# Cosine of the MLP input as a sine of the unfolded angle, with a bound from norms computed on the chip

## The chip, the cores and the metric

One core of one Trainium2 chip. The time is device microseconds of one launch: the median of three runs of the kernel before is 1383.35 us (1379.19 to 1383.68). The profile comes from one execution, whose span from first to last instruction is 1382.2 us, 1.15 us below that median. Engines are named as in the profile: PE (matmul, with PEld for its weight loads), DVE (vector), ACT (activation functions), POOL (GpSimd) and SP, which here issues DMAs only.

## What is computed

Three stages follow each other:

```python
# 1. attention, 4 batches x 8 heads, 576 positions, head size 64: only the 32 largest scores of a row count
scores = q @ k.T / 8;  kth = 32nd largest of each row
attn = softmax(scores where scores >= kth);  x = (attn @ v) laid out as 2304 tokens x 512
# 2. an MLP with an unusual activation
h = x @ w_in          # 2304 x 2048
g = h * np.cos(h)
x = g @ w_out         # 2304 x 512
# 3. eight experts, one per token (argmax of a gate), 512 -> 1024 -> 512
out[token] = gate_weight * eom * (relu(x @ w1[e]) @ w2[e])
```

The inputs fix the sizes that matter below: w_in is drawn as normal numbers divided by the root of 512, so a column of it has a squared length near 1 (its standard deviation is the root of 2/512, or 0.06), and a row of x is a mean of some 32 rows of v, which are normal numbers times 0.1, so its squared length is near 512 x 0.01 / 32 = 0.16.

## The kernel before

The work is a list of operations, each with its engine, an estimated duration, the values it reads and writes, and a due time (`prio`). A planner in the program (`Plan`) takes this list before launch, gives each engine the most urgent operation that can start by its own estimates, and writes one fixed order for every engine. On the chip each engine goes through its own order, in order, waiting on semaphores. The tags of the planner (`hs`, `rr`, `nn`, `ps` and so on) are sets of places in memory: an operation can start only when its value has a place.

Attention goes by 80 units: 64 main units (128 query rows of two heads) and 16 mixed ones (64 rows of two heads). In a unit PE makes the scores (L551), ACT copies them out of the banks (L557), DVE folds a row into maxima and minima of its halves (L580) and finds the 32nd largest value with MAX8 and MATCH_REPLACE8 (L585 to L600), POOL and ACT turn the rest into a large negative number (L604 to L618), ACT takes the exponential (L621), DVE makes the reciprocals and spreads them (L627, L629), and PE turns and multiplies with v (L641 to L682). The result, split into a high and a low part of reduced precision, goes into one of two places `xc`, a chunk of 256 tokens. There are 9 chunks.

As soon as a chunk is whole, the MLP runs on it, in 8 units of 256 tokens x 256 columns of w_in (72 units in all), interleaved with the attention of the next chunks. Each unit, `moe_unit`: 24 matmuls (L765 to L767; high x high, high x low, low x high), ACT copies the bank to `hs` (L771), POOL computes h/(2 pi) + 1/4 into `rr` (L773), DVE rounds that to an integer in `nn` by adding and subtracting a large constant (L775), POOL subtracts (L777). Units are collected in groups of up to four, and ACT takes the sine of 2 pi times the folded fraction of a whole group (L787), because exponential and sine need different tables, and each change of table shows as a load of 1283 ns. `moe_tail` then multiplies with h (DVE, L795), splits (ACT L806, POOL L808) and multiplies with w_out, whose tiles SP loads again and again from a scratch buffer (PE, L816 to L818). When the eighth unit of a chunk is done, `route` works out the expert of each token.

Beside this, in the first 330 us, the double-precision weights w_in and w_out are narrowed (L714 to L749) by DVE, ACT and POOL. The tag `nn` serves those too. After the last chunk, from about 1086 us on, the experts run; PE is busy nearly all of that stretch. A one-time check stands between the two: DVE reduces the flags of ties in the top 32 to one number per partition, PE adds it and the counts of tokens over the partitions (L1111, L1112), and DVE writes the result (L1116, L1117). At the very end a branch reads it: if a number exceeds the capacity, a slow general path recomputes what is needed, in plain loops that fold the angle as above.

Banks of PSUM: six are shared by everything before the experts (`ps`), two hold the w_out sums (`acc`).

Of the kernel before, what the change touches and what calls it, by code (L numbers as in the profile page):

```python
# [8 lines left out]
F32 = mybir.dt.float32  # L9
# [4 lines left out]
AF = mybir.ActivationFunctionType  # L14
OP = mybir.AluOpType
AX = mybir.AxisListType

P = 128
TOPK = 32
MAGIC = 12582912.0  # L20
INV_2PI = 0.15915494309189535
TWO_PI = 6.2831850
LOWEST = -3.0e38
MASK_GAIN = float(2.0 ** 90)
FAR = 1 << 20
# [41 lines left out]


class Buf:
    """A value in one of the places of its tag; the place is picked when the first op starts."""  # L70

    def __init__(self, tag, dt):
        self.tag = tag
# [11 lines left out]


class Plan:
    """Orders the ops of all engines: takes them in program order, finds what depends on what,
    and gives each engine the most urgent op that can start."""

    CROSS = 190.0
    SAME = {"PE": 0.0, "ACT": 130.0, "DVE": 130.0, "POOL": 130.0, "SP": 0.0}
# [4 lines left out]
        self.loose = set()  # L97

    def tag(self, name, places, loose=False, under=None):
        """`places`: (ap, area, first, last) each; `under`: tags whose last values must have left the place."""  # L100
        if loose:
            self.loose.add(name)
        self.tags[name] = []
        for ap, area, lo, hi in places:
            below = [(n, p) for n in under or () for p in self.tags[n] if p[3] == area and p[4] < hi and lo < p[5]]
            self.tags[name].append([ap, 0.0, True, area, lo, hi, below])
# [35 lines left out]
        return o  # L142

    def gone(self, slot):
        """When the values under a place are gone, or None."""
        t = slot[1]
        for n, p in slot[6]:
            if not p[2] or self.taken[n] < len(self.line[n]):
                return None
            t = max(t, p[1])  # L150
        return t

    def place(self, o, t):
        """When the places that `o` needs are free, or None."""
        need = {}
        for b in o.bufs:
            if b.tag and b.slot is None:
                need.setdefault(b.tag, []).append(b)
        for tag, bs in need.items():
            if tag not in self.loose:  # L160
                head = self.line[tag][self.taken[tag]:self.taken[tag] + len(bs)]
                if any(b not in head for b in bs):
                    return None
            free = sorted(f for f in (self.gone(s) for s in self.tags[tag] if s[2]) if f is not None)
            if len(free) < len(bs):
                return None
            t = max(t, free[len(bs) - 1])
        return t
# [78 lines left out]
def vec(n, psum=False):  # L247
    return 69.0 + n * (1.04 if psum else 1.042)


def fast(n):
    return 69.0 + n * 0.521
# [6 lines left out]
def pool(n):  # L259
    return 20.0 + n * 2.357  # L260


def pool_s(n):
    return 80.0 + n * 0.98
# [3 lines left out]
def tile_topk_attention_moe_moe2(ctx, tc, q, k, v, w_in, w_out, w_gate, w_ogate, w1, w2, out):  # L268
# [42 lines left out]
    seen = const.tile([P, E], F32, name="seen")  # L311
    nc.gpsimd.memset(seen, 0.0)
    spacer = const.tile([1, 1], F32, name="spacer")
    ebias = const.tile([P, 2], F32, name="ebias")
    nc.gpsimd.memset(ebias[:, 0:1], float(-EXP_OFF * 2 ** 23))
    nc.gpsimd.memset(ebias[:, 1:2], float(2 ** 20))

    tiles = []
    for b in range(B):
# [128 lines left out]
    plan.tag("ps", banks[0:6], loose=True)  # L448
    plan.tag("acc", banks[6:8])

    B_wg, B_table, B_x2d, B_seen, B_out = (plan.fixed() for _ in range(5))
    B_wod = plan.fixed()

    def dma(fn, nbytes, r=(), w=(), prio=0.0):
# [300 lines left out]

    def moe_unit(c, fp, prio):
        xc = XC[c]
        ph, hs, rr, nn = plan.buf("ps"), plan.buf("hs"), plan.buf("rr"), plan.buf("nn")
        for i in range(2):
            for c_ in range(KC):  # L760
                def mm(i=i, c_=c_):
                    o = ph.ap[:, i * CH:(i + 1) * CH]
                    fs = slice((2 * fp + i) * P, (2 * fp + i + 1) * P)
                    xh, xl = xc.ap
                    nc.tensor.matmul(o, w_in_h[:, c_, fs], xh[:, c_, :], start=(c_ == 0), stop=False)  # L765
                    nc.tensor.matmul(o, w_in_h[:, c_, fs], xl[:, c_, :], start=False, stop=False)  # L766
                    nc.tensor.matmul(o, w_in_l[:, c_, fs], xh[:, c_, :], start=False, stop=(c_ == KC - 1))  # L767

                plan.op({"PE": 327.0}, mm, [xc] + [(B_win, (fp // 2, c_, t)) for t in range(2)],
                        [ph], prio, hold=[hs])  # L770
        plan.op({"ACT": act(512, psum=True)}, lambda: nc.scalar.activation(hs.ap, ph.ap, AF.Copy),  # L771
                [ph], [hs], prio)
        plan.op({"POOL": pool_s(512)}, lambda: nc.gpsimd.tensor_scalar(  # L773
            rr.ap, hs.ap, INV_2PI, 0.25, op0=OP.mult, op1=OP.add), [hs], [rr], prio)
        plan.op({"DVE": fast(512)}, lambda: nc.vector.tensor_scalar(  # L775
            nn.ap, rr.ap, MAGIC, MAGIC, op0=OP.add, op1=OP.subtract), [rr], [nn], prio)
        plan.op({"POOL": pool(512)}, lambda: nc.gpsimd.tensor_tensor(rr.ap, rr.ap, nn.ap, op=OP.subtract),  # L777
                [nn], [rr], prio)
        group.append((c, fp, hs, rr, prio))
        if len(group) == SINS or (c, fp) in SIN_ENDS or (c, fp) == (NTILE // 2 - 1, UPC - 1):  # L780
            g = list(group)
            group.clear()
            rrs = [x[3] for x in g]

            def sins():
                for x in rrs:
                    nc.scalar.activation(x.ap, x.ap, AF.Sin, scale=TWO_PI)  # L787

            plan.op({"ACT": len(rrs) * 520.0}, sins, [], rrs, prio, kind="sin")
            for x in g:  # L790
                tail_at[0] = max(tail_at[0] + 10.0, prio + ADD["tail"])
                moe_tail(*x[:4], tail_at[0])

    def moe_tail(c, fp, hs, rr, prio):
        plan.op({"DVE": vec(512)}, lambda: nc.vector.tensor_tensor(rr.ap, hs.ap, rr.ap, op=OP.mult),  # L795
                [hs], [rr], prio)
        if fp == 0:
            ACC[c] = [plan.buf("acc"), plan.buf("acc")]
        acc = ACC[c]
        for i in range(2):  # L800
            f = 2 * fp + i
            ghl, wl = plan.buf("ghl"), plan.buf("wl", F32R)
            dma(lambda f=f, wl=wl: nc.sync.dma_start(shaped(wl.ap, 2, DM), wod[f]), P * 4096, r=[(B_wod, f)],
                w=[wl], prio=prio + 3 * i)
            gv = lambda i=i: rr.ap[:, i * CH:(i + 1) * CH]
            plan.op({"ACT": act(CH)}, lambda gv=gv, ghl=ghl: nc.scalar.activation(ghl.ap[:, 0], gv(), AF.Copy),  # L806
                    [rr], [(ghl, 0)], prio + 3 * i)
            plan.op({"POOL": pool(CH)}, lambda gv=gv, ghl=ghl: nc.gpsimd.tensor_tensor(  # L808
                ghl.ap[:, 1], gv(), ghl.ap[:, 0].bitcast(F32), op=OP.subtract), [rr, (ghl, 0)], [(ghl, 1)],
                prio + 3 * i)  # L810
            for t in range(2):
                def mm(f=f, t=t, ghl=ghl, wl=wl):
                    wr = lambda s: wl.ap[:, s * DM:(s + 1) * DM].bitcast(F32R)
                    ts_ = slice(t * P, (t + 1) * P)
                    gh, gl = ghl.ap[:, 0, ts_], ghl.ap[:, 1, ts_]
                    nc.tensor.matmul(acc[t].ap, gh, wr(0), start=(f == 0), stop=False)  # L816
                    nc.tensor.matmul(acc[t].ap, gh, wr(1), start=False, stop=False)  # L817
                    nc.tensor.matmul(acc[t].ap, gl, wr(0), start=False, stop=(f == NF - 1))  # L818

                plan.op({"PE": 648.0}, mm, [ghl, wl], [acc[t]], prio + 3 * i, hold=[acc[1 - t]])  # L820
        if fp == UPC - 1:
            route(c, prio + 1)
# [114 lines left out]
    for u in range(NU):  # L937
        if u in firsts:
            load_heads(*firsts[u], 10.0 * u - LOAD_AHEAD)
        attention(u)  # L940
        while todo and (u in chunk_done and todo[0] or len(pieces) - len(todo) < CONV_RATE * (u + 1)):
            f, a = todo.pop(0)
            f(*a, CONV_AT + 10.0 / CONV_RATE * (len(pieces) - len(todo)))
        if u in chunk_done:
            c = chunk_done[u]
            for fp in range(UPC):
                moe_unit(c, fp, 10.0 * (ready[c] + MOE_LAG) + MOE_STEP * fp)

# [146 lines left out]
    for e in range(E):  # L1095
# [10 lines left out]
            [B_flags], [B_worst], base)  # L1106
    plan.op({"DVE": 80.0}, lambda: nc.vector.tensor_scalar(
        worst[:, 1:2], worst[:, 0:1], 0.0, float(CAP + 1), op0=OP.is_ge, op1=OP.mult), [], [B_worst], base)

    def count():  # L1110
        nc.tensor.matmul(pc.ap[:, 0:E], ones, seen, start=True, stop=True)  # L1111
        nc.tensor.matmul(pc.ap[:, E:E + 1], ones, worst[:, 1:2], start=True, stop=True)  # L1112

    B_cnt = plan.fixed()
    plan.op({"PE": 120.0}, count, [B_seen, B_worst], [pc], base)
# [273 lines left out]
```

## Time and profile before

| | |
|---|---|
| median of three runs | 1383.35 us |
| profiled execution, span | 1382.2 us |
| PE busy | 1180.1 us, 85% |
| PE weight loads busy | 936.6 us, 68% |
| DVE busy | 988.5 us, 72% |
| ACT busy | 854.9 us, 62% |
| POOL busy | 885.2 us, 64% |
| first and last fold subtraction (L777) | 162.7 us, 1034.1 us |

Busy time is the union of an engine's instructions. Matmuls overlap each other, so their busy time and their single durations are longer than their spacing. In a list of groups, the columns are: line, engine, operation, output and input, shapes, count; then busy time in us and the mean of one in ns; then the idle time of the engine just before them and what ended it.

### The profile page before, as it was taken

What the parts mean: (1) busy time and instruction counts of PE and PEld (TensorE: products, weight loads), DVE (VectorE), ACT (ScalarE), POOL (GpSimd) and SP (SyncE); (2) the same over time, 40 slices, a digit from 0 to 9 for tenths busy, and PEclk for the clock granted to TensorE, in tenths of its full rate; (3) what the DMA queues carried; (4) which work ended last, traced back from release to release, by engine and by line L of the source; (5) the groups of instructions that cost most, each with busy time, mean ns of one, the idle gap of its engine ahead of it and who ended that gap; (6) DMA issues with size and microseconds to landing.
All of it is one profiled execution on the core that took longest, in us unless ns stands there. A gap on an engine that the chain in (4) does not pass through costs nothing.

```text
span 1382.2 us, 22655 instructions
## 1 busy us (share of the span) xinstructions
PE 1180.1 (85%) x7478; PEld 936.6 (68%) x7479; DVE 988.5 (72%) x2864; ACT 854.9 (62%) x1854; POOL 885.2 (64%) x1130
## 2 busy tenths in 40 slices
PE   3467778768898999999989898899994599999996
PEld 2334555547677668668767676767883599999995
DVE  6999999779599888999987889888335234444410
ACT  5777777767577787777766668767555244444421
POOL 6778888888666865776676657766765455555400
PEclk9655779989999989999999999999996699999998
DMA  8223323534440343323345321241557444444100
GB/s 210 76 107 113 98 67 116 182 131 162 144 139 8 111 140 105 122 92 104 96 135 152 100 78 36 89 137 46 174 184 267 166 160 158 149 156 160 58 17 23
DMA packets 95807, 164.72 MB, mean 119 GB/s; under 512 B 49850, under 2 KB 54202, under 8 KB 95680
## 3 DMA queue, kind: packets, MB, share of 16 engines
q1 hardware_dynamic: 91264, 153.71, 34.3%
q0 software_dynamic: 4416, 9.47, 2.1%
q8 instruction: 61, 1.00, 0.3%
q14 instruction: 66, 0.54, 0.1%
HBM read 146.72 MB, written 19.56 MB: 120 GB/s over the span
## 4 chain that ended last, share of the span: by engine, by line
PE 41%; DVE 29%; POOL 13%; issue 10%; ACT 6%; DMA 2%; POOLq 0%; DVEq 0%; ACTq 0%
DVE area_a L590 7%; DVE area_a L595 6%; DVE area_a L580 6%; PE bank L682 4%; PE bank L551 3%; PE bank L816 3%; PE bank L818 3%; PE bank L817 3%; PE bank L1052 2%; PE bank L1053 2%; PE bank L641 2%; PE bank L1054 2%; POOL area_a L618 2%; PE bank L765 2%; POOL area_g L777 2%
## 5 line engine op out<-in xcount | busy, mean ns | idle before, releaser
L590 DVE MAX8 area_a<-area_a 128x8 f32<-128x288 f32 x576 | 243.6, 444 | 1.1
L618 POOL TENSOR_TENSOR area_a<-area_a 128x576 f32<-128x576 f32 x144 | 195.8, 1368 | 23.0 <-ACT area_a L614 21.9
L595 DVE MATCH_REPLACE8 area_a<-area_a 128x288 f32<-128x288 f32 x432 | 187.8, 438 | 0.0
L580 DVE TENSOR_TENSOR area_a<-area_a 128x288 f32<-128x288 f32 x288 | 176.7, 639 | 14.5 <-ACT area_a L557 11.0
L765 PE MATMUL bank<-area_f,area_w 128*128 128x256 f32 x576 | 177.6, 308 | 2.3 <-ACT area_h L771 2.3
L641 PE MATMUL bank<-ident,area_a 128*128 128x128 f32 x576 | 104.5, 313 | 70.6 <-ACT area_a L621 57.8
L766 PE MATMUL bank<-area_f,area_w 128*128 128x256 f32 x576 | 163.3, 284 | 0.0
L767 PE MATMUL bank<-area_f,area_w 128*128 128x256 f32 x576 | 163.0, 283 | 0.0
L551 PE MATMUL bank<-area_a 64*128 64x288 f32 x512 | 133.3, 513 | 25.5 <-ACT area_a L541 22.5
L641 PEld LDWEIGHTS bank<-ident,area_a 128*128 128x128 f32 x576 | 73.8, 158 | 100.3 <-ACT area_a L621 78.4
L816 PE MATMUL bank<-area_l,area_f 128*128 128x512 f32 x288 | 130.4, 453 | 1.3 <-ACT area_f L806 0.6
L614 ACT ACTIVATE area_a<-area_a 128x576 bf16<-128x576 f32 x144 | 107.3, 768 | 37.5 <-POOL area_a L604 37.2
L808 POOL TENSOR_TENSOR area_f<-area_g,area_f 128x256 fp32r<-128x256 f32 x144 | 114.9, 811 | 23.7 <-ACT area_f L806 20.8
L777 POOL TENSOR_TENSOR area_g<-area_g,area_n 128x512 f32<-128x512 f32 x72 | 105.7, 1468 | 35.3 <-DVE area_a L600 14.8
L621 ACT ACTIVATE area_a<-area_a 128x576 f32<-128x576 f32 x144 | 111.2, 773 | 27.1 <-POOL area_a L618 26.2
L682 PE MATMUL bank<-area_a 128*64 128x128 f32 (+3 forms) x1600 | 123.3, 296 | 1.5 <-ACT area_a L662 1.3
L818 PE MATMUL bank<-area_l,area_f 128*128 128x512 f32 x288 | 119.7, 416 | 5.3 <-POOL area_f L808 5.0
L765 PEld LDWEIGHTS bank<-area_f,area_w 128*128 128x128 f32 x576 | 112.1, 195 | 14.2 <-issue 9.2
L682 PEld LDWEIGHTS bank<-area_a 128*64 128x64 f32 (+1 forms) x1600 | 89.8, 150 | 42.3 <-issue 18.3
L817 PE MATMUL bank<-area_l,area_f 128*128 128x512 f32 x288 | 118.2, 410 | 0.0
L766 PEld LDWEIGHTS bank<-area_f,area_w 128*128 128x128 f32 x576 | 111.8, 194 | 1.0
L767 PEld LDWEIGHTS bank<-area_f,area_w 128*128 128x128 f32 x576 | 111.0, 193 | 0.0
(197 smaller groups left out, 3005.4 us busy)
## 6 DMA issues: line engine op xcount, KB each, us to landing
area_l<-wod SPq DMA_DIRECT2D x144, 512.0 KB, 3.6
area_l<-in_moe_w_dram SPq DMA_DIRECT2D x52, 512.0 KB, 4.3
area_l<-in_moe_w_in_dram SPq DMA_DIRECT2D x16, 512.0 KB, 4.3
area_l<-in_moe_w_out_dram SPq DMA_DIRECT2D x16, 512.0 KB, 4.1
wod<-area_l SPq DMA_DIRECT2D x16, 512.0 KB, 2.6
area_n<-in_moe_w_dram SPq DMA_DIRECT2D x12, 512.0 KB, 4.9
area_a<-in_k_dram SPq DMA_DIRECT2D x32, 128.0 KB, 3.5
area_a<-in_q_dram SPq DMA_DIRECT2D x32, 128.0 KB, 3.4
```

The source lines that it names most:

```text
L551: nc.tensor.matmul(o.ap[:, 0:HALF], qt.ap[j * D:(j + 1) * D, :], kt.ap[j * D:(j + 1) * D, at:at + HALF], start=True, stop=True)
L580: plan.op(cost, lambda j=j, to=to, op=op, eng=eng: eng.tensor_tensor(to(), sc.ap[:, j, 0:HALF], sc.ap[:, j, HALF:S], op=op), [(sc, j)], [( ...
L590: lambda j=j, t=t: nc.vector.max(mx.ap[:, j, 8 * t:8 * t + 8], up.ap[:, j, :]),
L595: lambda j=j, t=t: nc.vector.match_replace(up.ap[:, j, :], mx.ap[:, j, 8 * t:8 * t + 8], up.ap[:, j, :], LOWEST),
L618: plan.op({"POOL": 1234.0}, lambda j=j: nc.gpsimd.tensor_tensor(sc.ap[:, j, :], sc.ap[:, j, :], bl.ap[:, j, :], op=OP.subtract), [(bl, j)] ...
L641: nc.tensor.transpose(pp.ap[:, r_ * P:(r_ + 1) * P], flat[:, at + r_ * P:at + (r_ + 1) * P], ident)
L682: nc.tensor.matmul(o.ap[j * D:(j + 1) * D, 0:w], lh, rh, start=(r_ == 0), stop=(r_ == R))
L765: nc.tensor.matmul(o, w_in_h[:, c_, fs], xh[:, c_, :], start=(c_ == 0), stop=False)
L766: nc.tensor.matmul(o, w_in_h[:, c_, fs], xl[:, c_, :], start=False, stop=False)
L767: nc.tensor.matmul(o, w_in_l[:, c_, fs], xh[:, c_, :], start=False, stop=(c_ == KC - 1))
L816: nc.tensor.matmul(acc[t].ap, gh, wr(0), start=(f == 0), stop=False)
L818: nc.tensor.matmul(acc[t].ap, gl, wr(0), start=False, stop=(f == NF - 1))
```

## The change

The fold goes: L773, L775 and L777 are no longer there. The sine of a group reads `hs` itself, with the constant pi/2 added inside the activation as a bias read from a column of `ebias`, and writes `rr`. A place of `rr` is therefore taken when the sines start, not when the fold starts, and `nn` is used by the narrowing of weights alone.

[...] New products make a bound: for each chunk, PE multiplies the two 128-token blocks of the high part of x with themselves (4 matmuls each), and DVE takes the largest element of each row; in chunks 1 to 4 the same is done for four 128-column blocks of w_in. The diagonals are squared lengths. With x below 1.60 and w below 1.50, |h| is at most the root of 2.4, 1.549. Two new comparisons in the one-time check send the launch to the general path otherwise; they are added by two more one-column matmuls into the sum that the branch reads. The general path itself stays as it was.

```diff
-    ebias = const.tile([P, 2], F32, name="ebias")
+    ebias = const.tile([P, 3], F32, name="ebias")
...
+    nc.gpsimd.memset(ebias[:, 2:3], HALF_PI)
+    norms = const.tile([P, 2, NTILE // 2], F32, name="norms")
+    nc.gpsimd.memset(norms, 0.0)
...
     def moe_unit(c, fp, prio):
         xc = XC[c]
-        ph, hs, rr, nn = plan.buf("ps"), plan.buf("hs"), plan.buf("rr"), plan.buf("nn")
+        ph, hs, rr = plan.buf("ps"), plan.buf("hs"), plan.buf("rr")
...
-        plan.op({"POOL": pool_s(512)}, lambda: nc.gpsimd.tensor_scalar(
-            rr.ap, hs.ap, INV_2PI, 0.25, op0=OP.mult, op1=OP.add), [hs], [rr], prio)
-        plan.op({"DVE": fast(512)}, lambda: nc.vector.tensor_scalar(
-            nn.ap, rr.ap, MAGIC, MAGIC, op0=OP.add, op1=OP.subtract), [rr], [nn], prio)
-        plan.op({"POOL": pool(512)}, lambda: nc.gpsimd.tensor_tensor(rr.ap, rr.ap, nn.ap, op=OP.subtract),
-                [nn], [rr], prio)
         group.append((c, fp, hs, rr, prio))
...
-            rrs = [x[3] for x in g]
+            hss, rrs = [x[2] for x in g], [x[3] for x in g]
 
             def sins():
-                for x in rrs:
-                    nc.scalar.activation(x.ap, x.ap, AF.Sin, scale=TWO_PI)
+                for h_, x in zip(hss, rrs):
+                    nc.scalar.activation(x.ap, h_.ap, AF.Sin, bias=ebias[:, 2:3])
 
-            plan.op({"ACT": len(rrs) * 520.0}, sins, [], rrs, prio, kind="sin")
+            plan.op({"ACT": len(rrs) * 613.0}, sins, hss, rrs, prio, kind="sin")
...
+    def gram(dst, n, cols, r, w, prio):
+        pg = plan.buf("ps")
+        def mm():
+            for i in range(n):
+                for c_, x in enumerate(cols(i)):
+                    nc.tensor.matmul(pg.ap[:, i * P:(i + 1) * P], x, x, start=(c_ == 0), stop=(c_ == KC - 1))
+        plan.op({"PE": KC * n * 110.0}, mm, r, [pg], prio)
+        plan.op({"DVE": vec(P * n, True)}, lambda: nc.vector.tensor_reduce(
+            dst, pg.ap[:, 0:P * n], axis=AX.X, op=OP.max), [pg], w, prio)
...
         if u in chunk_done:
             c = chunk_done[u]
+            gram(norms[:, 0, c:c + 1], 2, lambda i, c=c: [XC[c].ap[0][:, c_, i * P:(i + 1) * P] for c_ in range(KC)],
+                 [XC[c]], [(B_norms, ("x", c))], 10.0 * (ready[c] + MOE_LAG) + 1.0)
+            if 1 <= c <= 4:
+                fq = c - 1
+                gram(norms[:, 1, fq:fq + 1], 4, lambda i, fq=fq: [
+                    w_in_h[:, c_, (4 * fq + i) * P:(4 * fq + i + 1) * P] for c_ in range(KC)],
+                     [(B_win, (fq, c_, 0)) for c_ in range(KC)], [(B_norms, ("w", fq))],
+                     10.0 * (ready[c] + MOE_LAG) + 2.0)
...
+    plan.op({"DVE": 90.0}, lambda: nc.vector.tensor_reduce(worst[:, 2:4], norms, axis=AX.X, op=OP.max),
+            [B_norms], [B_worst], base)
+    for i, limit in ((2, X_LIMIT), (3, W_LIMIT)):
+        plan.op({"DVE": 80.0}, lambda i=i, limit=limit: nc.vector.tensor_scalar(
+            worst[:, i:i + 1], worst[:, i:i + 1], limit, float(CAP + 1), op0=OP.is_gt, op1=OP.mult),
+            [], [B_worst], base)
 
     def count():
         nc.tensor.matmul(pc.ap[:, 0:E], ones, seen, start=True, stop=True)
-        nc.tensor.matmul(pc.ap[:, E:E + 1], ones, worst[:, 1:2], start=True, stop=True)
+        for i in range(1, 4):
+            nc.tensor.matmul(pc.ap[:, E:E + 1], ones, worst[:, i:i + 1], start=(i == 1), stop=(i == 3))
```

Since the planner works on the whole list, the order of every engine is worked out anew; its due times and estimates for all other operations are the same.

## Rows read from the trace of the kernel before

**Rows 1.** Busy time of each engine by stretch; a header names the columns.
```profile
core 0: us, PE busy (x) PEld busy (x) DVE busy (x) ACT busy (x) POOL busy (x), PEclk, DMA share, GB/s
...
157.00:300.00 143.00, 105.92 (x666) 77.58 (x665) 122.27 (x329) 102.00 (x231) 121.25 (x143) 0.82 0.37 117
300.00:980.00 680.00, 628.52 (x4509) 484.61 (x4509) 590.45 (x1976) 491.47 (x1146) 464.56 (x656) 0.96 0.33 106
980.00:1040.00 60.00, 59.19 (x380) 51.69 (x379) 17.37 (x46) 28.27 (x54) 38.60 (x46) 1.00 0.59 194
1040.00:1086.00 46.00, 13.48 (x58) 10.77 (x56) 20.76 (x37) 20.60 (x24) 29.66 (x24) 0.57 0.78 279
```

**Rows 2.** The chain of work that ended last, shares of the whole span.
```profile
PE 41%; DVE 29%; POOL 13%; issue 10%; ACT 6%; DMA 2%; POOLq 0%; DVEq 0%; ACTq 0%
DVE area_a L590 7%; DVE area_a L595 6%; DVE area_a L580 6%; PE bank L682 4%; PE bank L551 3%; PE bank L816 3%; PE bank L818 3%; PE bank L817 3%; PE bank L1052 2%; PE bank L1053 2%; PE bank L641 2%; PE bank L1054 2%; POOL area_a L618 2%; PE bank L765 2%; POOL area_g L777 2%
```

**Rows 3.** Groups of POOL and DVE instructions between 157 and 1040 us.
```profile
L777 POOL TENSOR_TENSOR area_g<-area_g,area_n 128x512 f32<-128x512 f32 x72 | 105.7, 1468 | 35.3 <-DVE area_a L600 14.8 <-DVE area_n L775 8.9 <-DVE area_a L629 3.7
L773 POOL TENSOR_SCALAR area_g<-area_h 128x512 f32<-128x512 f32 x72 | 47.4, 659 | 33.8 <-ACT area_h L771 29.1
...
L580 DVE TENSOR_TENSOR area_a<-area_a 128x288 f32<-128x288 f32 x245 | 144.2, 614 | 12.5 <-ACT area_a L557 9.0 <-ACT area_a L571 3.4
L795 DVE TENSOR_TENSOR area_g<-area_h,area_g 128x512 f32<-128x512 f32 x72 | 56.5, 809 | 4.3 <-ACT area_g L787 4.3
L775 DVE TENSOR_SCALAR area_n<-area_g 128x512 f32<-128x512 f32 x72 | 33.1, 460 | 45.9 <-POOL area_g L773 45.8
L629 DVE COPY area_a<-area_a 128x128 f32<-128x128 f32 x71 | 28.2, 397 | 1.1 <-PE bank L653 0.9
```

**Rows 4.** Single lines, whole span: least, median and largest duration in ns.
```profile
L580 DVE TENSOR_TENSOR area_a<-area_a x288: 428/448/1557, 12.5 to 965.1; 128x288 f32<-128x288 f32 x144
L795 DVE TENSOR_TENSOR area_g<-area_h,area_g x72: 662/684/2187, 211.3 to 1036.5; 128x512 f32<-128x512 f32 x72
L629 DVE COPY area_a<-area_a x80: 199/219/1285, 37.3 to 979.0; 128x128 f32<-128x128 f32 x80
L721 ACT ACTIVATE area_n<-area_l,ebias x32: 736/756/782, 6.5 to 321.8; 128x512 f32<-128x512 uint32 x32
L724 ACT ACTIVATE area_g<-area_g x32: 612/626/636, 7.2 to 324.1; 128x512 f32<-128x512 int32 x32
```

**Rows 5.** Waits up to 1000 us: us in total, times, longest.
```profile
DVE area_n L775 <- POOL area_g L773: 25.6, 18, 5.1
...
PE bank L641 <- ACT area_a L621: 57.8, 44, 7.1
PE bank L653 <- DVE area_a L629: 33.5, 27, 3.5
PE bank L551 <- ACT area_a L541: 22.5, 8, 7.2
```

**Rows 6.** Timeline of PE: start us, duration us, engine, line, operation.
```profile
616.80 0.28 PE L765 MATMUL bank<-area_f,area_w 128*128 128x256 f32 x1
616.92 0.28 PE L766 MATMUL bank<-area_f,area_w 128*128 128x256 f32 x1
...
1061.96 0.59 PE L1111 MATMUL bank<-seen,ones 128*128 128x8 f32 x2 [1.94 <-DVE seen L907]
1062.40 0.56 PE L1112 MATMUL bank<-worst,ones 128*128 128x1 f32 x2
```

**Rows 7.** Groups of the whole span that stand near the added operations.
```profile
L641 PE MATMUL bank<-ident,area_a 128*128 128x128 f32 x576 | 104.5, 313 | 70.6 <-ACT area_a L621 57.8 <-ACT area_a L557 10.5 <-ACT area_a L541 1.2
...
L1035 DVE TENSOR_TENSOR area_f<-bank,area_f 128x512 fp32r<-128x512 f32 x24 | 15.9, 688 | 60.2 <-ACT area_f L1033 60.2
...
L865 DVE COPY area_t<-bank 128x32 f32<-128x32 f32 x9 | 1.7, 189 | 16.0 <-PE bank L848 16.0
```

More of the change, by code (lines that the diff above doesn't have):

```diff
@@ L22 @@
 TWO_PI = 6.2831850
+HALF_PI = 1.5707963267948966
+X_LIMIT = 1.60
+W_LIMIT = 1.50
 LOWEST = -3.0e38
@@ L449, in tile_topk_attention_moe_moe2 @@
     plan.tag("acc", banks[6:8])
-    B_wg, B_table, B_x2d, B_seen, B_out = (plan.fixed() for _ in range(5))
+    B_wg, B_table, B_x2d, B_seen, B_out, B_norms = (plan.fixed() for _ in range(6))
     B_wod = plan.fixed()
```

## The prediction

> **What bounds the kernel now.** I read the stretches first, because the change touches only those in which the MLP runs. From 157 to 1040 us the three first stretches [rows 1] add up to 883 us, with DVE busy 122.3 + 590.5 + 17.4 = 730 us (83%), POOL 624.4 us (71%), ACT 621.7 us (70%), and PE 793.6 us by its matmuls (90%) but 613.9 us by its weight loads (70%). In the 680 us in the middle DVE is at 87%. From 980 to 1040 us the attention is over, DVE falls to 29% and PE is busy 59.2 of 60 us: there only matmuls count. Before 157 us there is no fold to remove, and from 1086 us on the experts run, which the change leaves alone. So whatever comes, comes out of the middle.
>
> The chain of waits was second [rows 2]. It says that no engine holds the end alone: PE 41%, DVE 29%, POOL 13%, with the DVE search lines in front, and the fold subtraction L777 by itself at 2%, some 28 us. Next the groups of DVE and POOL [rows 3] beside the least and median durations of the same lines [rows 4]: L580 usually takes 448 ns and on average 614, so something else stretches it. Last the waits [rows 5].
>
> I take DVE as the bound between 157 and 980 us, with PE a close second, and POOL as the engine that slows DVE and feeds both late.
>
> **The change part by part.**
>
> *DVE loses L775.* 72 x 460 ns = 33.1 us [rows 3]. None of it lies beside other DVE work, so on the bound it counts whole: -33.
>
> *POOL loses L773 and L777.* 47.4 + 105.7 = 153.1 us of the 624.4 us that POOL is busy in the stretch [rows 1, 3], 24.5%. POOL isn't the bound, so this counts only by what it does to others, in two ways. First, the stretching of DVE. Busy time over count times median: L580 144.2 - 245 x 0.448 = 34.4 us, L629 28.2 - 71 x 0.219 = 12.7 us, L795 56.5 - 72 x 0.684 = 7.3 us, together 54 us [rows 3, 4]. If it goes with the time in which POOL works, 24.5% of it leaves: -13. The ends are 0 (the rest of POOL's work moves into the gaps and stretches as much as now) and twice that, -26 (a long operation like L777 stretches more than its share). I take the proportional value, since other POOL operations over 1 us, L618 above all, stay.
>
> Second, DVE waits for L773: 45.8 us in all [rows 3], of which 25.6 up to 1000 us [rows 5]; the rest is in the tail, where DVE has nothing to do anyhow. These waits go, but DVE then meets the next late thing, which will be matmul results and the scores. I count a quarter of the 25.6, -6; the ends are 0 and -26.
>
> *The new DVE reductions.* 9 of 256 columns and 4 of 512 columns, from a bank. The nearest rows are L1035, 512 columns from a bank, 688 ns, and L865, 32 columns, 189 ns [rows 7]: on the line between them 256 columns take 0.42 us. 9 x 0.42 + 4 x 0.69 = 6.6 us: +7. Ends: 13 x 0.19 = 2.5 and 13 x 0.69 = 9.0.
>
> *The new products on PE.* 9 x 8 + 4 x 16 = 136 matmuls of 128 columns. Reduced-precision matmuls of 256 columns start 0.12 us apart [rows 6]; 136 x 0.12 = 16 us. If each took a whole duration of the 128-column transposes, 313 ns [rows 7], it would be 43 us; below nothing no reason leads. The first row has the operand type and the array shape of the new ones, so I take 16. PE is on the chain for 41% of it [rows 2]: +7, ends 0 and 17. Every product also adds a wait: in PE's order it stands beside the matmuls of its chunk, which need the same x, so it should find its data ready; behind it queue the unit's matmuls and the attention's scores. It holds one of six banks until DVE has reduced it.
>
> *The sine with a bias from memory.* L721 reads such a bias and takes 756 ns where L724, the same size without one, takes 626 [rows 4]: 72 x 0.13 = 9.4 us on ACT, at most; at least 0. ACT is at 70% in the stretch and has 6% of the chain [rows 2]: +1. The number of table loads follows the grouping, which stays.
>
> *Places.* `rr` is taken later and `hs` let go earlier; the sine still needs all places of a group at once. I cost this at nothing. What covers it is that the tails drain the four `rr` places before the next group is collected; without that cover a group's sines would wait for a tail's split.
>
> *The check.* Two more products of the kind of L1112 start 0.44 us apart [rows 6], 0.9 us, ahead of the copy that stands before the last routing results; three DVE operations fall into a stretch where DVE is busy 20.8 of 46 us [rows 1]. +1. The tail from 980 to 1040 us gains nothing, since PE is full there.
>
> Sum: -33 - 13 - 6 + 7 + 7 + 1 + 1 = -36 us. The profiled span of 1382.2 gives 1346; the median of the runs lies 1.15 us above the span, so 1347 against 1383.35.
>
> *A rule that bears on PE.* The matmul rows say 90%, the weight-load rows 70% [rows 1]. The Trainium skill (Perfetto Trace Analysis, Identifying the Most-Contended Engine) holds that the busy share of matmuls is no good measure of TensorE's headroom and that the busy share of its weight loads is. By the rule DVE is the most contended engine and the sum stands; by the matmul rows PE is, and the first rival below comes out. The trace agrees with the rule in part: matmuls 0.12 us apart show 0.28 us each [rows 6], yet from 980 to 1040 us the weight loads show 86% where nothing else is left to bind.
>
> **The rivals.**
>
> *PE takes the bound (about 1365).* For it: PE's 90% and its 41% of the chain. Against: its weight loads, and that PE's largest waits are for others [rows 5]. Then only PE waits that end on a late DVE shrink, L653 on L629, 33.5 us [rows 5], and the new products count whole, 16: -33.5 + 16 = -18.
>
> *POOL was the hidden brake (about 1318).* PE waits 57.8 us for the exponential L621 [rows 5], which comes after L618 on POOL; L773 and L777 stand in the same queue as L618, and POOL has 13% of the chain. With a quarter of POOL's work gone, half of that wait could go too: -36 - 29 = -65. Against: most of those waits follow the top-32 search on DVE, which POOL doesn't shorten.
>
> *Slower: PE stands at the head of its queue (about 1408).* The order of PE is fixed, and 13 new products stand in it. If one comes before its chunk or its narrowed weights are there by the clock of the chip (the planner's estimates leave out the stretching of DVE), everything behind it waits. PE's waits of this kind reach 7.1 and 7.2 us now [rows 5]. At 5 us each, 13 x 5 = 65, less 36 of gain, plus some drift: +25 to +30. It decides from 36 / 13 = 2.8 us each. Against: the units right behind ask for the same data, so the wait would mostly have been there anyway.
>
> *No difference.* The new order of all engines, made with due times that were set for the other list, could lose just what is saved. Nothing in the rows speaks for such an accident.
>
> *It doesn't do what it says.* If a norm went over its limit, the general path would recompute all, far over 1000 us more, since the DVE search alone costs hundreds of us even now. Squared lengths near 0.16 against 1.60, and near 1 with a deviation of 0.06 against 1.50, which is eight deviations, leave no room for that: 0.01, kept inside the slower case.
>
> **How the numbers follow.** Forecast (1330 to 1358) 0.44; PE bound (1358 to 1379) 0.22; POOL brake (1300 to 1330) 0.20; no difference 0.05; slower 0.09. About 0.3%, or 4.2 us, is what a measurement of this kernel can tell from none: faster is 0.44 + 0.22 + 0.20 = 0.86, same 0.05, slower 0.09. The range goes down to 1308, so that it takes in most of the brake case and the far ends of stretching and waits (-26 + 13, -26 + 6: 33 us below 1347 is 1314), and up to 1378: left out are 0.14 above and some 0.05 below.
>
> **What would show it.** No instruction at L773, L775 and L777's places; POOL busy down by about 150 us, DVE by about 40; the median of L580 unchanged and its mean nearer to it; sines of some 0.75 us; the stretch from the first MLP unit to the last shorter by about 36 us, the experts as long as before. PE waiting for L621 much less would speak for the brake; a PE busy share that rises while DVE's falls, for the first rival; long PE waits right before the new products, for the slower one. The forecast is wrong if DVE's busy time falls as said and the span doesn't follow.

## The result and the profile after

The changed kernel takes 1349.71 us (median of four, 1346.87 to 1352.61) against 1381.27 us for the kernel before: ratio 0.9772, 95% interval 0.9748 to 0.9796, or 32 us less. The profiled execution has a span of 1345.2 us against 1382.2. One of the four launches of the run m4_old_list below went at a lower granted clock (0.80) and took 1408 us; its time in the table is the median of the other three.

Busy time by stretch in the changed kernel; the columns are those of [rows 1]:

```profile
core 0: us, PE busy (x) PEld busy (x) DVE busy (x) ACT busy (x) POOL busy (x), PEclk, DMA share, GB/s
...
0.00:157.00 157.00, 95.04 (x470) 62.42 (x472) 136.59 (x370) 109.03 (x244) 118.44 (x160) 0.76 0.43 130
157.00:300.00 143.00, 118.99 (x795) 88.50 (x794) 124.89 (x347) 109.09 (x243) 107.27 (x133) 0.84 0.40 123
300.00:900.00 600.00, 560.50 (x4116) 433.89 (x4115) 515.38 (x1766) 445.78 (x1044) 308.59 (x495) 0.98 0.35 110
900.00:960.00 60.00, 57.83 (x443) 48.52 (x442) 42.40 (x149) 48.20 (x102) 27.32 (x47) 1.00 0.39 123
960.00:1000.00 40.00, 40.00 (x267) 36.46 (x266) 10.27 (x32) 20.86 (x37) 19.34 (x22) 1.00 0.66 225
1000.00:1050.00 50.00, 22.09 (x103) 17.87 (x103) 16.14 (x35) 18.25 (x26) 24.82 (x23) 0.68 0.72 246
1050.00:1345.00 295.00, 281.05 (x1436) 253.77 (x1435) 97.38 (x112) 104.25 (x159) 117.14 (x111) 0.97 0.32 107
```

From the first expert matmul to the end it takes as long as before (1052.8 to 1345.2 us here, 1089.3 to 1382.2 there). The last spreading copy of the attention (L629 before, L635 now) starts at 946.7 us instead of 979.0: 32 of the 37 us of span are gained before that point, in the middle, as the forecast had it. The gain does not grow evenly in the new order: the 26th of the 80 spreading copies comes 20 us earlier than before (343.8 against 363.9 us), the 61st 26 us. From 300 to 900 us DVE is still at 86%, with POOL down to 51%.

The busy times of the whole span, from the page of the changed kernel:

```profile
PE 1175.5 (87%) x7618; PEld 941.4 (70%) x7619; DVE 943.0 (70%) x2808; ACT 855.5 (64%) x1852; POOL 722.9 (54%) x988
```

DVE is busy 45.5 us less and POOL 162.3 us less than before.

Single lines of the changed kernel, answering to [rows 4] and, for the new operations, to [rows 6, 7]: least, median and largest duration in ns.

```profile
L586 DVE TENSOR_TENSOR area_a<-area_a x288: 427/448/1597, 12.5 to 933.9; 128x288 f32<-128x288 f32 x144
...
L635 DVE COPY area_a<-area_a x80: 196/216/1282, 37.3 to 946.7; 128x128 f32<-128x128 f32 x80
...
L787 ACT ACTIVATE area_g<-area_h,ebias x72: 705/709/726, 199.6 to 1002.1; 128x512 f32<-128x512 f32 x72
...
L804 DVE TENSOR_REDUCE norms<-bank x13: 398/425/678, 38.6 to 958.3; 128x1 f32<-128x256 f32 x9, 128x1 f32<-128x512 f32 x4
```

The sines take 709 ns each; before, without the bias, their median was 616 ns. So the bias costs 93 ns a sine, 6.7 us of durations in all, though ACT's busy time as a whole is 855.5 us against 854.9. The Trainium skill (ScalarE: Activation LUTs, What ACT_TABLE_LOAD costs) gives some 93 ns for an operand read per partition; the trace agrees. The median of the folds is 448 ns as before.

Waits in the changed kernel up to 963 us, answering to [rows 5]: us in total, times, longest.

```profile
DVE area_a L694 <- PE bank L688: 40.1, 26, 5.8
DVE area_a L586 <- ACT area_a L563: 20.8, 17, 2.7
...
PE bank L647 <- ACT area_a L627: 31.0, 28, 3.9
PE bank L659 <- DVE area_a L635: 28.1, 24, 3.8
PE bank L557 <- ACT area_a L547: 11.9, 4, 6.6
```

PE waits for the exponential (L627, before L621) 31.0 us instead of 57.8. The prediction had named that as the mark of the "brake" rival. DVE's wait for the fold is gone, and its waits for products of PE and for copied scores have grown in its place: 40.1 and 20.8 us, where they were 29.9 and 11.0.

### The profile page after: what moved, and what is told of

Its sections match the earlier page's. It is cut to its first block, busy times and chain, and to the rows that moved or that the text cites. A ratio compares the mean times of both kernels' runs of the same rounds, so it can differ in the third digit from the quotient of the medians.

```text
span 1345.2 us, 22640 instructions
## 1 busy us (share of the span) xinstructions
PE 1175.5 (87%) x7618; PEld 941.4 (70%) x7619; DVE 943.0 (70%) x2808; ACT 855.5 (64%) x1852; POOL 722.9 (54%) x988
## 5 line engine op out<-in xcount | busy, mean ns | idle before, releaser
L586 DVE TENSOR_TENSOR area_a<-area_a 128x288 f32<-128x288 f32 x288 | 172.9, 625 | 28.1 <-ACT area_a L563 20.8
L773 PE MATMUL bank<-area_f,area_w 128*128 128x256 f32 x576 | 161.9, 281 | 0.0
L821 POOL TENSOR_TENSOR area_f<-area_g,area_f 128x256 fp32r<-128x256 f32 x144 | 111.0, 786 | 77.9 <-ACT area_f L819 58.0
L647 PE MATMUL bank<-ident,area_a 128*128 128x128 f32 x576 | 96.9, 296 | 57.7 <-ACT area_a L627 31.0
L557 PE MATMUL bank<-area_a 64*128 64x288 f32 x512 | 124.1, 492 | 12.9 <-ACT area_a L547 11.9
L829 PE MATMUL bank<-area_l,area_f 128*128 128x512 f32 x288 | 127.8, 444 | 0.4 <-ACT area_f L819 0.2
L647 PEld LDWEIGHTS bank<-ident,area_a 128*128 128x128 f32 x576 | 68.8, 149 | 84.4 <-ACT area_a L627 46.7
L627 ACT ACTIVATE area_a<-area_a 128x576 f32<-128x576 f32 x144 | 111.5, 774 | 18.5 <-POOL area_a L624 16.9
L771 PEld LDWEIGHTS bank<-area_f,area_w 128*128 128x128 f32 x576 | 110.9, 192 | 15.5 <-issue 11.6
L831 PE MATMUL bank<-area_l,area_f 128*128 128x512 f32 x288 | 116.0, 403 | 1.3 <-POOL area_f L821 1.3
L830 PE MATMUL bank<-area_l,area_f 128*128 128x512 f32 x288 | 116.1, 403 | 0.0
L772 PEld LDWEIGHTS bank<-area_f,area_w 128*128 128x128 f32 x576 | 110.7, 192 | 2.4 <-POOL area_f L710 1.3
L610 POOL TENSOR_SCALAR area_a<-area_a 128x2 f32<-128x2 f32 (+1 forms) x80 | 32.9, 412 | 147.2 <-DVE area_a L606 132.1
L773 PEld LDWEIGHTS bank<-area_f,area_w 128*128 128x128 f32 x576 | 109.8, 191 | 0.0
```

What stands on the lines that cost most here:

```text
L557: nc.tensor.matmul(o.ap[:, 0:HALF], qt.ap[j * D:(j + 1) * D, :], kt.ap[j * D:(j + 1) * D, at:at + HALF], start=True, stop=True)
L586: plan.op(cost, lambda j=j, to=to, op=op, eng=eng: eng.tensor_tensor(to(), sc.ap[:, j, 0:HALF], sc.ap[:, j, HALF:S], op=op), [(sc, j)], [( ...
L647: nc.tensor.transpose(pp.ap[:, r_ * P:(r_ + 1) * P], flat[:, at + r_ * P:at + (r_ + 1) * P], ident)
```

## The experiments

Two kinds of run. In the first the planner made a new order for each kernel. In the second the list of operations stayed as it was, and some of them simply issued nothing when their turn came, so that every engine kept its order. The times stand with their ratio to the kernel before on the same chip; the chips differ between groups of runs, so the ratios compare best. DVE busy and span are of the profiled execution.

| run | us | ratio, 95% interval | DVE busy | span |
|---|---|---|---|---|
| before | 1381.27 | | 988.5 | 1382.2 |
| changed | 1349.71 | 0.9772, 0.9748 to 0.9796 | 943.0 | 1345.2 |
| *new order* | | | | |
| e1_no_norms | 1353.71 | 0.9790, 0.9756 to 0.9825 | 954.3 | 1352.2 |
| e2_dve_back | 1371.06 | 0.9910, 0.9874 to 0.9945 | 986.5 | 1371.2 |
| e3_pool_back | 1375.10 | 0.9947, 0.9926 to 0.9969 | 993.1 | 1375.7 |
| e4_fold_unused | 1383.11 | 1.0001, 0.9981 to 1.0021 | 1002.1 | 1382.8 |
| *kept order* | | | | |
| o1_norms_not_issued | 1338.56 | 0.9685, 0.9665 to 0.9704 | 938.7 | 1336.7 |
| o2_fold_not_issued | 1337.49 | 0.9674, 0.9651 to 0.9697 | 934.2 | 1336.6 |
| o3_pool_not_issued | 1346.41 | 0.9738, 0.9709 to 0.9768 | 956.2 | 1344.4 |
| o4_dve_not_issued | 1361.27 | 0.9853, 0.9825 to 0.9882 | 967.0 | 1359.2 |
| q1_pool_writes | 1349.28 | 0.9805, 0.9759 to 0.9852 | 941.3 | 1340.9 |
| *tried as better versions* | | | | |
| m1_product_pool | 1343.77 | 0.9749, 0.9718 to 0.9780 | 925.5 | 1338.9 |
| m4_old_list | 1353.70 | 0.9823, 0.9782 to 0.9863 | 944.6 | 1350.9 |
| m5_w_late | 1354.79 | 0.9816, 0.9781 to 0.9851 | 949.6 | 1353.9 |

### The norms taken out, with a new order

```diff
-            gram(norms[:, 0, c:c + 1], 2, ...)
-            if 1 <= c <= 4:
-                gram(norms[:, 1, fq:fq + 1], 4, ...)
...
-    (the reduction of norms and the two comparisons)
```

> The changed kernel without the new products, their reductions and the two new comparisons (it leaves the bound on |h| out). Theory of the forecast (DVE is the bound, PE close behind): the 6.6 us of DVE, 7 us of PE and 1 us of the check come back, so about 1336 us against 1350 for the changed kernel. Rival (the products run in gaps of PE and only DVE counts): about 1343. Rival (the norms are hidden altogether): 1350.

It came out no faster than the changed kernel, at 1353.7 us, above all three expectations. DVE was busy 11 us longer although 7 us of its work were gone. That couldn't be the price of the norms alone, and it raised the question of the order, which the kept-order run o1 below answers.

### DVE's part put back, POOL's part put back, both put back

```diff
+        nn = plan.buf("nn")                      # e2: 72 roundings on DVE
+        plan.op({"DVE": fast(512)}, lambda: nc.vector.tensor_scalar(
+            nn.ap, hs.ap, MAGIC, MAGIC, op0=OP.add, op1=OP.subtract), [hs], [nn], prio)
...
+        nn = plan.buf("nn")                      # e3: 144 operations on POOL
+        plan.op({"POOL": pool_s(512)}, lambda: nc.gpsimd.tensor_scalar(
+            nn.ap, hs.ap, INV_2PI, 0.25, op0=OP.mult, op1=OP.add), [hs], [nn], prio)
+        plan.op({"POOL": pool(512)}, lambda: nc.gpsimd.tensor_tensor(nn.ap, nn.ap, hs.ap, op=OP.subtract),
+                [hs], [nn], prio)
```

e4 is e1 with the three operations in a row, in place in `nn`.

> The changed kernel with 72 rounding operations of DVE put back (same shape and form as the removed L775, reading hs, writing a place nobody reads). Theory of the forecast (33 us of DVE count whole): about 1380 us, all of the gain gone. Rival (POOL was the brake, DVE has slack): 1350 to 1358. In the trace: DVE busy up by about 33 us in either case.

> The changed kernel with 144 POOL operations put back (72 of the form of L773, 72 of the form of L777, reading hs, writing a place nobody reads, so that nothing waits for them). Theory of the forecast (POOL counts by stretching DVE, 13 us, and by waits that are not rebuilt here): about 1363 us. Rival (POOL was the hidden brake through the queue before L618): 1380 to 1395. Rival (POOL is free): 1350. The trace tells by the mean of L586, 625 ns in the changed kernel: towards 640 by the theory.

> The changed kernel without the norms, with the whole fold put back (POOL, DVE, POOL in a row, in a place of nn) but not between h and the sine: the sine reads hs with the bias, nobody reads the fold. It leaves the bound on |h| out. Theory of the forecast (the work on the engines is what cost, not the chain through them): within 8 us of the kernel before, 1373 to 1385 us. Rival (the cost was the chain of waits between matmul and sine): near the run without norms, about 1340.

DVE's part put back cost 21 us, POOL's 25. Both times lie between the theories that had been set (1380 against at most 1358 for e2; 1363 against at least 1380 for e3), so neither theory of a single brake holds: each part alone takes back most of the gain. The traces moved more than expected. In e2 the roundings themselves took 41 us, not 33, and DVE was busy 43.5 us longer:

```profile
L780 DVE TENSOR_SCALAR area_n<-area_h 128x512 f32<-128x512 f32 x72 | 41.2, 573 | 31.8 <-ACT area_h L777 31.8
```

In e3 DVE was busy 50.1 us longer with no work of its own added, and a fold took 666 ns on average, past the 640 of the theory. In e4 no sine waits for the fold, and it is still as slow as the kernel before. That speaks for the work on the engines as the cost, and not the chain of waits through the fold. But e2, e3 and e4 each have a new order, and a new order alone can be worth 15 us (next section), so these three runs don't price a part by themselves.

### The same parts in a kept order

```diff
-        plan.op({"POOL": pool_s(512)}, lambda: nc.gpsimd.tensor_scalar(rr.ap, hs.ap, ...), [hs], [rr], prio)
+        plan.op({"POOL": pool_s(512)}, lambda: None, [hs], [rr], prio)          # o2, o3
...
-        plan.op({"DVE": fast(512)}, lambda: nc.vector.tensor_scalar(nn.ap, rr.ap, ...), [rr], [nn], prio)
+        plan.op({"DVE": fast(512)}, lambda: None, [rr], [nn], prio)             # o2, o4
...
-                    nc.scalar.activation(x.ap, x.ap, AF.Sin, scale=TWO_PI)
+                    nc.scalar.activation(x.ap, h_.ap, AF.Sin, bias=ebias[:, 2:3])
```

(the subtraction on POOL likewise; o1 does the same with the norms in the changed kernel.)

> The changed kernel in exactly its own order on every engine, with the instructions of the norms and of the two new comparisons not issued (it leaves the bound on |h| out). Theory A (the norms cost what the forecast gave them, and the run without norms lost that again to a worse new order): 1335 to 1342 us. Theory B (the norms are hidden, and what the run without norms lost was no matter of order): 1348 to 1354.

> The kernel before in exactly its own order on every engine, with the fold's 216 instructions not issued and the sine reading hs with the bias (no norms, so it leaves the bound on |h| out). Theory A (the removed work is the gain, the new order is worth nothing): 1335 to 1350 us. Theory B (the gain needs the new order, which uses the freed time): 1360 to 1375.

> The kernel before in its own order, with only the 144 POOL instructions of the fold not issued; the 72 DVE roundings stay, reading hs, off the path of the sine (no norms, no bound on |h|). From the runs with work put back, in which DVE's 33 us cost 21: 1358 to 1370 us by the theory that DVE work and POOL work both count. Rival (POOL's work counts only beside the chain of waits through it): under 1350.

> The kernel before in its own order, with only the 72 DVE roundings not issued; the 144 POOL instructions stay (the second reads hs in place of the rounded value), and the sine still waits for them to have written its place (no norms, no bound on |h|). From the run with POOL's work put back, which cost 25 us: 1362 to 1376 us. DVE busy down by 30 to 35 us against the kernel before. Rival (only DVE's own work counts): about 1350.

o1 and e1 hold the same instructions and differ by 15 us, which is order. In o1 the norms cost 11 us (1349.71 - 1338.56). o2 reaches 1337.5 us in the old order: a new order isn't needed for the gain, and is worth about nothing here (o1 against o2: 1 us). o3 missed its theory (1358 to 1370 us): at 1346.4 us it lies where the rival had it, by which POOL's work counts only beside the chain of waits through it. o3 takes away both, so it can't tell them apart. o4 came out at 1361.3 us, just under its range, though DVE busy fell by 21.5 us, not 30 to 35.

DVE groups of o2, o3 and o4, whole span: the folds of the attention (the halves of a row, not the angle), the products h times sine (L794 in o2, L795 in o3) and the spreading copies. First o2, with no work on the angle at all:

```profile
L581 DVE TENSOR_TENSOR area_a<-area_a 128x288 f32<-128x288 f32 x288 | 169.6, 616 | 18.2 <-ACT area_a L558 11.2 <-ACT area_a L572 6.9
...
L794 DVE TENSOR_TENSOR area_g<-area_h,area_g 128x512 f32<-128x512 f32 x72 | 51.7, 744 | 19.4 <-ACT area_g L786 19.3
...
L630 DVE COPY area_a<-area_a 128x128 f32<-128x128 f32 x80 | 25.2, 314 | 1.2 <-PE bank L654 0.9
```

o3, the DVE roundings kept:

```profile
L581 DVE TENSOR_TENSOR area_a<-area_a 128x288 f32<-128x288 f32 x288 | 163.3, 593 | 15.1 <-ACT area_a L558 9.9 <-ACT area_a L572 5.1
...
L795 DVE TENSOR_TENSOR area_g<-area_h,area_g 128x512 f32<-128x512 f32 x72 | 52.1, 750 | 6.7 <-ACT area_g L787 6.6
...
L775 DVE TENSOR_SCALAR area_n<-area_h 128x512 f32<-128x512 f32 x72 | 36.8, 511 | 27.3 <-ACT area_h L772 26.1 <-POOL area_l L750 1.2
...
L630 DVE COPY area_a<-area_a 128x128 f32<-128x128 f32 x80 | 25.0, 313 | 0.9 <-PE bank L654 0.7
```

o4, the POOL operations kept:

```profile
L581 DVE TENSOR_TENSOR area_a<-area_a 128x288 f32<-128x288 f32 x288 | 179.7, 651 | 14.7 <-ACT area_a L558 8.7 <-ACT area_a L572 5.8
...
L630 DVE COPY area_a<-area_a 128x128 f32<-128x128 f32 x80 | 35.9, 448 | 0.4
```

And the kernel before, whole span:

```profile
L580 DVE TENSOR_TENSOR area_a<-area_a 128x288 f32<-128x288 f32 x288 | 176.7, 639 | 14.5 <-ACT area_a L557 11.0 <-ACT area_a L571 3.4
...
L629 DVE COPY area_a<-area_a 128x128 f32<-128x128 f32 x80 | 33.8, 423 | 1.1 <-PE bank L653 0.9
```

The same instructions, and their time follows POOL: with POOL's operations on the angle away, the folds take 163 and 170 us and the copies 25; with them, 177 and 180 us, and 34 to 36.

### POOL busy as long, but only writing

```diff
-        (o4's first POOL operation of a unit)   nc.gpsimd.tensor_scalar(rr.ap, hs.ap, ...)
+        nc.gpsimd.memset(rr.ap, 0.0)
-        (o4's second)                           nc.gpsimd.tensor_tensor(rr.ap, rr.ap, hs.ap, op=OP.subtract)
+        [nc.gpsimd.memset(rr.ap, 0.0) for _ in range(3)]
```

> The run with only the DVE roundings not issued (kernel before's order, 1361 us), with its 144 POOL operations that read memory replaced by 288 fills of 128x512 in the same places of POOL's order, one for the first operation of a unit and three for the second; a fill reads nothing. By the fills of other sizes in the changed kernel's trace (204 ns for 128 columns, 338 ns for 288) a fill of 512 columns should take some 0.55 us, so POOL is busy about as long as before (no norms, no bound on |h|). Theory A (POOL's work cost time by holding up DVE operations that read two operands, and fills don't do that): 1337 to 1347 us, with the excess of the folds L581 over their median near the 41 us of the run without any fold work, not 51. Theory B (POOL's work cost time by standing in POOL's queue before L618): 1357 to 1365 us.

The groups of DVE and, last, one of the two groups of fills on POOL:

```profile
L581 DVE TENSOR_TENSOR area_a<-area_a 128x288 f32<-128x288 f32 x288 | 168.3, 611 | 17.0 <-ACT area_a L558 10.4 <-ACT area_a L572 6.4
...
L630 DVE COPY area_a<-area_a 128x128 f32<-128x128 f32 x80 | 33.2, 415 | 1.8 <-PE bank L654 1.4
```

```profile
L776 POOL MEMSET area_g<- 128x512 f32 x216 | 114.1, 528 | 9.9
```

POOL is busy 869.4 us, as in o4 (871.5), but the folds take 168.3 us: 288 x 0.448 from that leaves 39.3 us of stretching, about as without POOL's work on the angle (40.6 in o2), not 50.7 as in o4. The copies stay stretched, 33.2 us. The Trainium skill (SBUF — State Buffer, Who interferes with whom) says that a vector instruction with two inputs in SBUF is held up by a GpSimd instruction that reads SBUF, not by one that only writes, while a copy in a mode that uses both ports is held up by either. The trace agrees for the folds, and for the copies if they run in such a mode, which no run here shows.

The time is inconclusive: 1349 us lies between the two theories, its interval overlaps o4's, and its four launches run from 1342.6 to 1357.3. The trace is that of the fastest launch. In it POOL's queue is as full as in o4 and the sine still waits for POOL, yet the span of 1340.9 us is 4.3 us above o2's and 18.3 below o4's. Nor does PE wait longer for the exponential than with POOL's part away. Waits up to 1000 us in o3, o4 and q1, in this order (57.8 in the kernel before, 41.9 in o2):

```profile
PE bank L642 <- ACT area_a L622: 45.3, 34, 7.1
PE bank L642 <- ACT area_a L622: 49.3, 37, 6.6
PE bank L642 <- ACT area_a L622: 44.2, 33, 6.3
```

### Versions that might be better

m1 moves the product h times sine from DVE to POOL; m4 adds the norms to the old list, with the fold planned but issuing nothing; m5 moves the products of w_in into the gap before the experts, the order before that kept.

```diff
-        plan.op({"DVE": vec(512)}, lambda: nc.vector.tensor_tensor(rr.ap, hs.ap, rr.ap, op=OP.mult),
+        plan.op({"POOL": pool(512)}, lambda: nc.gpsimd.tensor_tensor(rr.ap, hs.ap, rr.ap, op=OP.mult),   # m1
...
+    for fq in range(4):                                                                              # m5
+        gram(norms[:, 1, fq:fq + 1], 4, ..., [...] + [(B_x2d, (NTILE // 2 - 1, 0, 0))], ..., 0.9e5)
```

> The changed kernel with the product h times sine moved from DVE to POOL (72 operations: 54 us off DVE, about 100 us onto POOL). By the fixed-order runs a us of DVE busy time is worth 0.8 to 1 us, and 134 us of POOL's work were worth 24 to 35: so -43 to -54 for DVE, +18 to +27 for POOL, and +-15 for the new order: 1310 to 1340 us. Rival (POOL's reading work stretches DVE by as much as DVE gives away): 1345 to 1365.

> The norms added to the kernel before's list, which keeps the fold as planned operations that issue nothing, so that the planner spaces the work as before; the sine reads hs with the bias. It computes what the changed kernel computes. Theory (the norms cost 11 us and the order is a draw of some +-8 us): 1341 to 1357 us. Rival (the old spacing is better than the new one): under 1341.

> The changed kernel in its own order, with the four products of w_in moved out of the middle and into the gap before the experts, where PE is busy 22 of 50 us. Of the 11 us that the norms cost in this order, the 64 matmuls and four reductions of w_in make about half by count: 1343 to 1346 us if the gap hides them, 1346 to 1352 if they hold up the routing there.

m1, DVE's folds and POOL's products:

```profile
L586 DVE TENSOR_TENSOR area_a<-area_a 128x288 f32<-128x288 f32 x288 | 186.2, 673 | 43.4 <-ACT area_a L563 27.4 <-ACT area_a L577 16.0
```

```profile
L808 POOL TENSOR_TENSOR area_g<-area_h,area_g 128x512 f32<-128x512 f32 x72 | 93.1, 1306 | 25.4 <-ACT area_g L787 24.7
```

m1 is the fastest that still computes all, 1343.8 us, but its interval (0.9718 to 0.9780) overlaps that of the changed kernel. It falls between its two expectations: DVE gave away 54 us and is busy only 17.5 us less. Of the 36.5 us between, 13.3 are the folds, which stretched further (186.2 against 172.9); the rest is not broken down here. m4 lies where the theory of a drawn order put it. m5 missed: its attention ends where it did (last copy at 947.2 us), and its experts begin 10 us later, at 1062.7 us, where the changed kernel had 1052.8. So in the profiled executions moving the products of w_in away saved nothing in the middle and cost in the gap.

## Why the prediction was right, and where its terms were not

The sum said 36 us, and 32 were measured (37 between the two profiled spans). It is right by its place and its sign. That the size came out so near is luck: its two largest terms erred against each other. In the kept order:

| step | forecast | measured |
|---|---|---|
| DVE loses L775 | -33 | -20 alone (o4), -9 after POOL's part (o2 - o3) |
| POOL loses L773, L777 (stretching -13, waits -6) | -19 | -35 alone (o3), -24 after DVE's part (o2 - o4) |
| both | -52 | -44 (o2) |
| norms and check (+7 +7 +1), sine's bias (+1) | +16 | +11 for norms and check (o1); the bias not by itself |
| places, new order | 0 | about 1 (o1 against o2) |
| sum | -36 | -32 |

**"DVE loses L775 ... it counts whole" was too large.** Nor is it so that none of it lies beside other DVE work: the durations of neighbours on DVE overlap. In the kernel before:

```profile
601.14 0.40 DVE L775 TENSOR_SCALAR area_n<-area_g 128x512 f32<-128x512 f32 x1
601.46 0.21 DVE L629 COPY area_a<-area_a 128x128 f32<-128x128 f32 x1
```

The rounding shows 0.40 us, and the next instruction starts 0.32 us after it. Over all 72, only 25 of the 33 us are covered by no other DVE instruction (DVE's busy time is 988.5 us with them and 963.5 without). In o4 the folds and copies also took 3.0 and 2.1 us longer (179.7 against 176.7, 35.9 against 33.8), and DVE busy fell by 21.5 (988.5 to 967.0), the time by 20.0. The term should have been taken from spacings, as was done for PE.

**"The stretching goes with POOL's share, -13" was too small.** With POOL's operations away, folds, copies and products of the MLP take 176.7 + 33.8 + 56.5 - 163.3 - 25.0 - 52.1 = 26.6 us less, which is the upper end that was given (-26); in o2 it is 20.5. The 54 us of stretching that the term started from were low too: they set durations that overlap against a busy time that counts no overlap twice. By the means of [rows 3] it is 245 x 0.166 + 71 x 0.178 + 72 x 0.125 = 62 us. DVE busy fell by 32.3 us in o3 though every one of its instructions was kept, and the time by 34.9. How much of the 34.9 is the chain of waits, which the forecast priced at 6, was not measured by itself. In the changed kernel the same three lines took 15.7 us less (172.9, 24.4, 54.0).

**"I take DVE as the bound" held.** In the kept order, DVE busy less by 21.5, 32.3 and 54.3 us gave 20.0, 34.9 and 43.8 us of time. The last gives less time for its DVE work than the first two. From 157 us to the last spreading copy, a stretch of 822 us in the kernel before and 777 in o2, DVE's busy time falls by 49 us (712.1 to 662.7) and the stretch by 45: there the time still follows DVE, which is idle for some 5 us more. The other 5 us of its work leave stretches in which it does not bind. In new orders a us of DVE's busy time was worth less, about half: 43.5 and 50.1 us more cost 21 and 25 in e2 and e3.

**The rivals.** PE as the bound did not come: PE's work grew by 140 matmuls and the time fell by more than that rival's 18 us; but PE's weight loads are now busy 482.4 of 660 us from 300 to 960 us beside DVE's 557.8, so it stays second. The brake was half right: POOL was worth more than the forecast gave it, and PE's wait for the exponential fell by 26.8 us. That it acted through the queue before L618 wasn't shown. In the kept order that wait fell by 12.5 us with POOL's part away (o3), and by as much, 13.6, with POOL's queue full of fills (q1), which speaks against it; q1's time leaves it open. The slower rival didn't come: PE's waits before the new products are 1.8 and 1.1 us. The general path was not taken. The limits on the norms keep |h| under 1.549, and so h + pi/2 between 0 and pi; what the sine does beyond pi, no run here shows.

**The new products** took some 20 us of PE by their starts, where the forecast counted 16. Near 957 us, at a granted clock of 1.00 (2.4 GHz), eight of x took 0.84 us, and near 188 us sixteen of w_in 1.84, about as forecast. But near 73 us, at a granted clock of 0.50 (1.2 GHz), the products of w_in start 0.21 us apart, and sixteen near 35 us took 3.45 us.

**What stays open.** Why e1's order is 15 us worse than o1's with the same instructions: DVE is busy 954.3 against 938.7 us, and of these 15.6 us the folds (182.2 against 173.7) and the products h times sine (56.5 against 50.9) are 14.1. Both read two operands, so it looks as if more of them met POOL's operations; that was not shown, nor tried whether a planner could avoid it. Likewise why m5's middle gained nothing.

## What to carry to other kernels

Work taken off an engine that isn't the bound can be worth more than work taken off the bound, when the two get in each other's way: look at the mean of a line beside its median, and multiply. Count what an engine gives back by the spacing of its instructions, not by their durations. And where a planner remakes the whole order for each edit, first run the edit with the order kept; here a new order of the same instructions was worth 15 us, half of the change. When two errors cancel in a sum, the total says nothing of the terms: price each by a run that takes it away alone.

## What the runs showed of the hardware that had not been expected

POOL fills of 128x512, which only write, left the two-input DVE folds at 611 ns on average, where as much POOL time in reading operations had 651 ns; the one-input copies stayed at 415 ns (448, and 314 with neither). A POOL product of 128x512 took 1306 ns on average, its DVE twin 685 ns by the median and 785 on average beside POOL's work, so that giving it to POOL freed 17.5 us of DVE for 80.3 us of POOL.
